# A GFNet filter and MLP on one core: the first layer's result read once from PSUM, and a reordered last step

## The chip, the core and the metric

The kernel runs on one core of one Trainium2 chip. Its engines are TensorE (PE; the weight loads are listed as PEld), VectorE (DVE), ScalarE (ACT), GpSimd (POOL) and the queue engine SyncE (SP), which issues the DMAs. The metric is the device time of one execution in microseconds (us); lower is better.

## The reference

`x` has 2048 rows of 576 numbers in float32. What must be computed is a residual spectral filter, then a residual MLP:

```python
h  = x + irfft2(rfft2(layernorm(x)) * (w_r + 1j * w_i))      # over rows and columns
h2 = h + relu(layernorm(h) @ w1) @ w2                        # w1: 576 x 4608, w2: 4608 x 576
```

## The kernel before

The first part, up to about 270 us, does the Fourier filter as matrix products. The change does not touch it. The second part is the MLP. Its rows are split into `NC` = 4 groups (c) of 512 rows, and its 4608 hidden columns into `NG` = 18 groups (g) of 256. One pair (g, c) is a step; there are 72, in the order of `steps`. Every step adds its part of the second layer to `xs` (tile A in the profile), which holds h and becomes the output.

Full precision is kept by splitting: a number v is written as a high part h (rounded to the matmul type fp32r) and a low part l = v - h, and a product takes three matmuls (h by h, h by l, l by h). The helper `split(h, l, v)` does this with an ACT copy (L151) and a DVE subtraction (L307). `relu_split` (L534) does it straight from PSUM, with the ReLU: an ACT read (L536) and a DVE operation that reads PSUM too (L537).

From step 8 (`WINO`) on, the second layer of a step uses a Strassen-Winograd scheme with seven products instead of eight, of 256 x 128 by 128 x 288 blocks. The hidden block is 256 columns by 512 rows: `p0` and `p1` are its two 128-column halves, after the ReLU, each with 512 rows in two blocks of 256. The left operands are A11 = `p0[:, 0]`, A12 = `p1[:, 0]`, A22 = `p1[:, 1]`, and the sums S1 to S4, which POOL computes from p0 and p1 (L547, L551 to L553). Each left operand is split.

`slot(i)` writes out step i of this kind. TensorE's order is: quarter 0, products A11 and A12, quarter 1, products S2 and S1, quarter 2, products S3 and S4, quarter 3, product A22. A quarter is seven matmuls of the first layer of the *next* step (`mm1`, L148), so that the next step's hidden block is ready when this step ends; after quarters 1 and 3, `hid_a` (L542) reads the finished half from PSUM and starts the sums. A product is six matmuls (`prod`, L562), and after each of them DVE adds the sum so far into one or two blocks of `xs` (`add`, L569).

PSUM holds four tiles `wps`. `wps[0]` takes the products A11, S2, S3 and A22, one summed upon the other, with an add after each; `wps[1]` takes A12, then S1 and S4 upon each other. `wps[2]` and `wps[3]` hold the first layer's halves p0 and p1, one step in the lower and the next in the upper 512 columns. A product that opens or continues a sum in a tile waits for the add that last read this tile.

The kernel's order is written by hand: each engine executes its instructions in the order in which the program lists them, and semaphores join the engines. The second half of `hid_a` stands in quarter 3, thus ahead of the A22 product and its add; in DVE's queue the low part of A12 stands ahead of the A22 add. The last group of hidden columns also stores the output: `store` issues two DMAs on SP for every finished quarter block.

Of the kernel before, what the change touches and what calls it, by code (L numbers as in the profile page):

```python
# [12 lines left out]
AF = mybir.ActivationFunctionType  # L13
ALU = mybir.AluOpType
# [9 lines left out]
CH = 4  # L24
# [103 lines left out]
def kernel(ctx: ExitStack, tc: tile.TileContext, x, w_r, w_i, w1, w2, cc2, c1, fb, ib, c3, out):  # L128
    nc = tc.nc
# [3 lines left out]
    def sb(shape, tag, bufs=1, dt=F32):  # L133
        n[0] += 1
        return pool.tile(shape, dt, tag=tag, name=f"{tag}_{n[0]}", bufs=bufs)

    n = [0]

    def ps():
        n[0] += 1  # L140
        return psum.tile([128, 1024], F32, tag="d", name=f"d_{n[0]}", bufs=4)
# [8 lines left out]
    def act(o, i, **kw):  # L150
        nc.scalar.activation(o, i, AF.Copy, **kw)  # L151

    xs = sb([128, NT, D], "X")
    xv = x[0].rearrange("(h j t) d -> j h t d", j=2, t=NT)
    ov = out[0].rearrange("(h j t) d -> j h t d", j=2, t=NT)
# [149 lines left out]
    def split(h, l, v):  # L305
        act(h, v)
        nc.vector.tensor_sub(l, v, h)  # L307
# [3 lines left out]
    def work(k):  # L311
        for _ in range(k):
            split(*pieces.pop(0))
# [75 lines left out]
    xs = sb([128, NT, D], "A")  # L389
# [70 lines left out]
    def mm1(i, a, part=None):  # L460
        g, c = steps[i]
        w1h, w1l = wts[g, 0]
        if a == 0 and not part:
            pend[i] = None if i >= WINO else ps()
        p = hid_p(i, a) if i >= WINO else pend[i][:, 512 * a:512 * a + 512]
        f = slice(128 * a, 128 * a + 128)
        ops = []
        for kt in range(4):
            ops += [(w1h, kt, kt), (w1h, kt, 5 + kt), (w1l, kt, kt)]
        ops += [(w1h, 4, 4), (w1l, 4, 4)]  # L470
        for n_, (w, kt, xk) in enumerate(ops):
            if part is None or n_ // 7 == part:
                mm(p, w[:, kt, f], xc[c][:, xk, :], n_ == 0, n_ == len(ops) - 1)
        if i >= WINO:
            return
        if a == GF - 1:
            p = pend.pop(i).rearrange("p (a s) -> p a s", a=GF)
            hh, hl = sb([128, GF, 512], "D", 4, F32R), sb([128, GF, 512], "D", 4, F32R)
            nc.scalar.activation(hh, p, AF.Relu)
            nc.vector.scalar_tensor_tensor(hl, p, 0.0, hh, op0=ALU.max, op1=ALU.subtract)  # L480
            hid[i] = (hh, hl)
# [22 lines left out]
    wps, fs = [], {}  # L504
    NAMES = ("B22", "T4", "B11", "B21", "T2", "T1", "T3")

    def wform(n):
        o = 6208 + 576 * NAMES.index(n)
        return tail[0][:, o:o + 288], tail[0][:, o + 288:o + 576]

    def wino_sums(g, *ns):
        v = raw[g][1]
        if 1 in ns:
            T = ebuf([128, 4, 288])
            fs["T1"], fs["T2"], fs["T3"], fs["T4"] = (T[:, i] for i in range(4))
            fs["B11"], fs["B12"], fs["B21"], fs["B22"] = v[:, 0, :288], v[:, 0, 288:], v[:, 1, :288], v[:, 1, 288:]
        for n_ in ns:
            o, a, b = (("T1", "B12", "B11"), ("T2", "B22", "T1"), ("T3", "B22", "B12"), ("T4", "B21", "T2"))[n_ - 1]
            nc.gpsimd.tensor_sub(fs[o], fs[a], fs[b])

    def wino_w(*names):
        for n in names:
            split(*wform(n), fs[n])
# [7 lines left out]
        fs.update(S12f=(D3[:, 0:2], D3[:, 2:4]), S1f=(D3[:, 0], D3[:, 2]), S2f=(D3[:, 1], D3[:, 3]))  # L531
        fs.update(S3f=(tail[0][:, 5696:5952], tail[0][:, 5952:6208]))

    def relu_split(f, p):  # L534
        h, l = f
        nc.scalar.activation(h, p, AF.Relu)  # L536
        nc.vector.scalar_tensor_tensor(l, p, 0.0, h, op0=ALU.max, op1=ALU.subtract)  # L537

    def hid_p(i, k):
        return wps[2 + k][:, 512 * (i % 2):512 * (i % 2) + 512]  # L540

    def hid_a(i, k):  # L542
        p = hid_p(i, k)
        if k == 0:
            relu_split(fs["A11"], p[:, :256])
            nc.scalar.activation(fs["p0"], p.rearrange("p (a n) -> p a n", a=2), AF.Relu)  # L546
            nc.gpsimd.tensor_sub(fs["S3"], fs["p0"][:, 0], fs["p0"][:, 1])  # L547
        else:
            relu_split(fs["A12"], p[:, :256])
            nc.scalar.activation(fs["p1"], p.rearrange("p (a n) -> p a n", a=2), AF.Relu)  # L550
            nc.gpsimd.tensor_add(fs["S1"], fs["p0"][:, 1], fs["p1"][:, 1])  # L551
            nc.gpsimd.tensor_sub(fs["S2"], fs["S1"], fs["p0"][:, 0])  # L552
            nc.gpsimd.tensor_sub(fs["S4"], fs["p1"][:, 0], fs["S2"])  # L553

    def prod(i, a, b, bank, first):
        ah, al = fs[a]
        bh, bl = wform(b)
        P = wps[bank].rearrange("p (a n) -> p a n", a=2)[:, :, :288]
        for tt in range(2):
            q = slice(128 * tt, 128 * tt + 128)  # L560
            for n_, (l, r) in enumerate(((ah, bh), (ah, bl), (al, bh))):
                nc.tensor.matmul(P[:, tt], l[:, q], r, start=first and n_ == 0, stop=n_ == 2, skip_group_check=not first)  # L562

    def add(i, bank, *to):
        c = steps[i][1]
        P = wps[bank].rearrange("p (a n) -> p a n", a=2)[:, :, :288]
        for hs, hd in to:
            xt = xs[:, CH * c + 2 * hs:CH * c + 2 * hs + 2, 288 * hd:288 * hd + 288]
            nc.vector.tensor_add(xt, xt, P)  # L569

    def store(c, hs, hd):
        if steps[-1][0] == NG - 1:
            for j in range(2):
                t, d = CH * c + 2 * hs, slice(288 * hd, 288 * hd + 288)
                nc.sync.dma_start(ov[j, :, t:t + 2, d], xs[64 * j:64 * j + 64, t:t + 2, d])

    def slot(i):
        g, c = steps[i]
        more, last, turn = i + 1 < len(steps), g == NG - 1, c == NC - 1 and g < NG - 1
        new, w1 = c == 0 and g > 2, g < NG - 1 and c in (1, 2)  # L580

        def quarter(k):
            if more:
                mm1(i + 1, k // 2, k % 2)
                if k % 2:
                    hid_a(i + 1, k // 2)

        quarter(0)
        if new:
            wino_w("T3", "B22")  # L590
        if w1:
            work(1)
        prod(i, "A11", "B11", 0, True)
        add(i, 0, (0, 0))
        prod(i, "A12", "B21", 1, True)
        split(*fs["S12f"], fs["S12"])
        add(i, 1, (0, 0))
        if w1:
            wino_sums(g + 1, *((1, 3) if c == 1 else (2, 4)))
        if last:  # L600
            store(c, 0, 0)
        quarter(1)
        prod(i, "S2f", "T2", 0, False)
        add(i, 0, (0, 1))
        split(*fs["S4f"], fs["S4"])
        prod(i, "S1f", "T1", 1, True)
        add(i, 1, (1, 1))
        if turn:
            wino_w("B11", "B21")
        if w1:  # L610
            work(1)
        if new:
            wino_w("T4")
        quarter(2)
        prod(i, "S3f", "T3", 0, False)
        add(i, 0, (1, 1))
        if last:
            store(c, 1, 1)
        if more:
            split(*fs["S3f"], fs["S3"])  # L620
        prod(i, "S4f", "B22", 1, False)
        add(i, 1, (0, 1))
        if turn:
            wino_w("T2", "T1")
        if w1 and c == 1:
            work(1)
        if last:
            store(c, 0, 1)
        quarter(3)
        prod(i, "A22", "T4", 0, False)  # L630
        add(i, 0, (1, 0))
        if more:
            relu_split(fs["A22"], hid_p(i + 1, 1)[:, 256:])
        if last:
            store(c, 1, 0)

    first = [(0, 0), (0, 1), (0, 2), (1, 0), (1, 1), (0, 3), (1, 2), (1, 3)]
    steps = first + [(g, c) for g in range(2, NG) for c in range(NC)]

    gen = None  # L640
    for t in range(NT + 6):
# [15 lines left out]
        if 10 <= t < 22:  # L657
            i, u = divmod(t - 10, 4)
# [15 lines left out]
    for i in range(3, len(steps)):  # L674
        if i + 5 < len(steps) and steps[i + 5] == (steps[i + 5][0], 0):
            load_weights(steps[i + 5][0])
        if i + 3 < len(steps) and steps[i + 3] == (steps[i + 3][0], 0):
            split_weights(steps[i + 3][0], 0)
        if i == WINO - 3:
            wino_sums(2, 1, 2, 3, 4)  # L680
        if i == WINO - 2:
            wino_w("B11", "B21", "T2", "T1", "T3")
        if i == WINO - 1:
            wps += [None, None, ps(), ps()]
            wino_tiles()
        if i == WINO:
            wps[:2] = ps(), ps()
        if i >= WINO:
            slot(i)
            continue  # L690
        for a in range(GF):
            mm1(i + 1, a)
            if i == WINO - 1:
                hid_a(i + 1, a)
        for tt in range(CH):
            mm2(i, tt)
        if i == WINO - 1:
            relu_split(fs["A22"], hid_p(i + 1, 1)[:, 256:])
            split(*fs["S3f"], fs["S3"])
            wino_w("B22", "T4")  # L700

# [21 lines left out]
```

## Time and profile before

| | |
|---|---|
| median of 3 runs | 1055.14 us (1054.94 to 1055.36) |
| profiled execution, its own time | 1053.18 us |
| its span, first to last instruction | 1051.1 us, granted TensorE clock 0.999 |
| TensorE busy | 1033.6 us (98%) |
| DVE busy | 751.3 us (71%) |
| ACT busy | 389.9 us (37%) |
| POOL busy | 325.7 us (31%) |

In the rows of the timeline the columns are: start in us from the span's start, length in us, engine, line, operation, tiles (out <- in), shapes, count, and in brackets the idle time of the engine before the row and what ended it. In the groups of instructions the numbers behind the bar are busy time in us and the mean of one in ns, and behind the next bar the idle time before them. A row of the table of windows has the stretch, its length and the busy time of each engine. PEld rows are the weight loads that go with the matmuls. The tile letters are the program's tags: A is `xs`, d any PSUM tile, D the split left operands, X the split weights and S3's parts, e the float32 tiles p0, p1, S1 to S4 and the raw weights, B and C the first layer's right operand.

### The profile page before, as it was taken

To read this page: it belongs to the slowest core of one execution; us is meant where nothing else is said; L and a number is where in the kernel's file an instruction comes from. 1 tells how busy PE (TensorE), PEld (TensorE's weight loads), DVE (VectorE), ACT (ScalarE), POOL (GpSimd) and SP (SyncE) were. 2 spreads that over 40 slices of the span, in tenths; PEclk is the share of its full clock that TensorE was granted. 3 is DMA by queue.
4 is the path that set the end of the run, shared out by engine and by line. 5 is a ranking of instruction groups with operands and counts; after the bars stand their busy time and mean duration, and the time that the engine had idled before them with its cause. 6 is when DMAs were issued, how large, how long until landed. Compare 5 with 4: busy or idle time off the path is not lost.

```text
span 1051.1 us, 17190 instructions
## 1 busy us (share of the span) xinstructions
PE 1033.6 (98%) x6560; PEld 924.6 (88%) x6560; DVE 751.3 (71%) x1411; ACT 389.9 (37%) x846; POOL 325.7 (31%) x436
## 2 busy tenths in 40 slices
PE   8999999999999999999999999999999999999997
PEld 7878778799999999999999999999999999999996
DVE  7587686544377777778777777778777777777775
ACT  4533243521134333333333333334343333434332
POOL 4300164311132324333333423333333323243321
PEclk9999999999999999999999999999999999999999
DMA  8931700011000110000000011000000001000025
GB/s 241 249 89 49 181 2 26 23 48 49 1 26 23 28 47 23 26 23 26 23 26 23 26 30 42 26 23 26 24 26 23 26 24 46 29 23 2 1 63 118
DMA packets 31073, 48.05 MB, mean 46 GB/s; under 512 B 2960, under 2 KB 22672, under 8 KB 30992
## 3 DMA queue, kind: packets, MB, share of 16 engines
q1 hardware_dynamic: 30992, 46.96, 16.3%
q8 instruction: 52, 0.85, 0.3%
q14 instruction: 29, 0.24, 0.1%
HBM read 42.23 MB, written 4.72 MB: 45 GB/s over the span
## 4 chain that ended last, share of the span: by engine, by line
PE 94%; DVE 2%; DMA 2%; ACT 1%; POOL 0%; issue 0%; SPq 0%; ACTq 0%; DVEq 0%; POOLq 0%
PE d L148 59%; PE d L562 34%; DMA A<-in_A_x_dram 2%; PE d L446 1%; DVE st L208 0%; DVE A L428 0%; ACT e L222 0%; DMA X<-in_A_x_dram 0%; SPq L159 0%; DVE e L307 0%; POOL r L212 0%; DVE e L252 0%; PE d L447 0%; DVE e L253 0%; DVE e L416 0%
## 5 line engine op out<-in xcount | busy, mean ns | idle before, releaser
L569 DVE TENSOR_TENSOR A<-A,d 128x576 f32<-128x576 f32 x448 | 334.5, 747 | 50.5 <-PE d L562 50.2
L562 PE MATMUL d<-X,D 128*128 128x288 f32 x2304 | 346.2, 294 | 1.4 <-DVE A L569 0.9
L562 PEld LDWEIGHTS d<-X,D 128*128 128x128 f32 x2304 | 329.0, 188 | 17.2 <-DVE A L569 1.1
L148 PE MATMUL d<-B,e 128*128 128x512 f32 x952 | 238.3, 391 | 0.4 <-DVE A L428 0.4
L148 PEld LDWEIGHTS d<-B,e 128*128 128x128 f32 x952 | 172.0, 188 | 28.7 <-ACT e L151 0.8
L537 DVE SCALAR_TENSOR_TENSOR D<-d,D 128x256 fp32r<-128x256 f32 x192 | 81.5, 424 | 122.0 <-ACT D L536 122.0
L536 ACT ACTIVATE D<-d 128x256 fp32r<-128x256 f32 x192 | 73.4, 382 | 239.6 <-PE d L148 239.6
L551 POOL TENSOR_TENSOR e<-e 128x256 f32<-128x256 f32 x64 | 47.3, 739 | 355.3 <-ACT e L550 355.3
L148 PE MATMUL d<-C,e 128*128 128x512 f32 x476 | 119.1, 390 | 0.0
L148 PE MATMUL d<-X,e 128*128 128x512 f32 x476 | 118.8, 390 | 0.0
L151 ACT ACTIVATE X<-e 128x288 fp32r<-128x288 f32 (+2 forms) x177 | 70.2, 434 | 105.6 <-PE d L562 105.6
L307 DVE TENSOR_TENSOR D<-e,D 128x512 fp32r<-128x512 f32 (+1 forms) x128 | 92.7, 724 | 19.9 <-ACT D L151 19.9
L547 POOL TENSOR_TENSOR e<-e 128x256 f32<-128x256 f32 x64 | 47.6, 744 | 173.6 <-ACT e L546 173.6
L148 PEld LDWEIGHTS d<-X,e 128*128 128x128 f32 x476 | 85.9, 188 | 13.7
L148 PEld LDWEIGHTS d<-C,e 128*128 128x128 f32 x476 | 85.8, 188 | 13.7
L151 ACT ACTIVATE D<-e 128x512 fp32r<-128x512 f32 (+1 forms) x128 | 66.7, 521 | 75.5 <-POOL e L552 71.9
L307 DVE TENSOR_TENSOR X<-e,X 128x288 fp32r<-128x288 f32 (+2 forms) x177 | 83.1, 492 | 0.9 <-ACT X L151 0.9
L562 PEld LDWEIGHTS d<-X 128*128 128x128 f32 x384 | 58.0, 188 | 5.1
L562 PE MATMUL d<-X 128*128 128x288 f32 x384 | 61.4, 295 | 0.0
L148 PE MATMUL d<-e,D 128*128 128x288 f32 x384 | 53.8, 297 | 0.3 <-DVE D L480 0.3
L148 PEld LDWEIGHTS d<-e,D 128*128 128x128 f32 x384 | 52.2, 188 | 1.4 <-DVE D L480 0.6
L552 POOL TENSOR_TENSOR e<-e,e 128x256 f32<-128x256 f32 x64 | 50.4, 788 | 5.0
(79 smaller groups left out, 986.9 us busy)
## 6 DMA issues: line engine op xcount, KB each, us to landing
e<-in_B_w_dram SPq DMA_DIRECT2D x18, 576.0 KB, 3.8
e<-in_B_w_dram SPq DMA_DIRECT2D x18, 512.0 KB, 3.6
A<-in_A_x_dram SPq DMA_DIRECT2D x16, 288.0 KB, 8.4
out_dram<-A SPq DMA_DIRECT2D x32, 144.0 KB, 2.5
X<-in_A_x_dram SPq DMA_DIRECT2D x12, 288.0 KB, 7.1
e<-in_B_w_dram SPq DMA_DIRECT2D x36, 64.0 KB, 3.4
B<-in_A_w_r_dram SPq DMA_DIRECT2D x15, 144.5 KB, 8.1
B<-in_A_w_i_dram SPq DMA_DIRECT2D x15, 144.5 KB, 7.0
```

What stands on the lines that cost most here:

```text
L148: nc.tensor.matmul(o, l, r, start=start, stop=stop)
L151: nc.scalar.activation(o, i, AF.Copy, **kw)
L307: nc.vector.tensor_sub(l, v, h)
L446: nc.tensor.transpose(pz[:, 128 * b:128 * b + 128], y[:, 128 * b:128 * b + 128], ident)
L536: nc.scalar.activation(h, p, AF.Relu)
L537: nc.vector.scalar_tensor_tensor(l, p, 0.0, h, op0=ALU.max, op1=ALU.subtract)
L547: nc.gpsimd.tensor_sub(fs["S3"], fs["p0"][:, 0], fs["p0"][:, 1])
L551: nc.gpsimd.tensor_add(fs["S1"], fs["p0"][:, 1], fs["p1"][:, 1])
L552: nc.gpsimd.tensor_sub(fs["S2"], fs["S1"], fs["p0"][:, 0])
L562: nc.tensor.matmul(P[:, tt], l[:, q], r, start=first and n_ == 0, stop=n_ == 2, skip_group_check=not first)
L569: nc.vector.tensor_add(xt, xt, P)
```

## The change

Three things change.

1. The first layer's result is read from PSUM once per half. `hid_a` now lets ACT write p0 (or p1), all 512 columns with the ReLU, and A11 and A12 are split from that SBUF tile with `split`; A22 likewise, later in the step. `relu_split` is gone.
2. In the step before the last (`late`), quarter 3 stands directly behind quarter 2, ahead of the S3, S4 and A22 products; the splits of A22 and S3 for the last step stand at its end.
3. In the last step the products that went to `wps[0]` go to `wps[2]` (`X = 2`). Its last add is made in two halves, each with two stores of its own, so four stores of half the size take the place of two.

```diff
-    def relu_split(f, p):
-        h, l = f
-        nc.scalar.activation(h, p, AF.Relu)
-        nc.vector.scalar_tensor_tensor(l, p, 0.0, h, op0=ALU.max, op1=ALU.subtract)
...
         if k == 0:
-            relu_split(fs["A11"], p[:, :256])
             nc.scalar.activation(fs["p0"], p.rearrange("p (a n) -> p a n", a=2), AF.Relu)
+            split(*fs["A11"], fs["p0"][:, 0])
             nc.gpsimd.tensor_sub(fs["S3"], fs["p0"][:, 0], fs["p0"][:, 1])
         else:
-            relu_split(fs["A12"], p[:, :256])
             nc.scalar.activation(fs["p1"], p.rearrange("p (a n) -> p a n", a=2), AF.Relu)
+            split(*fs["A12"], fs["p1"][:, 0])
...
-    def add(i, bank, *to):
+    def add(i, bank, *to, tt=slice(0, 2)):
...
+        late, X = i + 2 == len(steps), 0 if i + 1 < len(steps) else 2
...
-        prod(i, "A11", "B11", 0, True)
-        add(i, 0, (0, 0))
+        prod(i, "A11", "B11", X, True)
+        add(i, X, (0, 0))
...
         quarter(2)
-        prod(i, "S3f", "T3", 0, False)
-        add(i, 0, (1, 1))
+        if late:
+            quarter(3)
+        prod(i, "S3f", "T3", X, False)
+        add(i, X, (1, 1))
         if last:
             store(c, 1, 1)
-        if more:
+        if more and not late:
             split(*fs["S3f"], fs["S3"])
...
-        quarter(3)
-        prod(i, "A22", "T4", 0, False)
-        add(i, 0, (1, 0))
+        if not late:
+            quarter(3)
+        prod(i, "A22", "T4", X, False)
         if more:
-            relu_split(fs["A22"], hid_p(i + 1, 1)[:, 256:])
-        if last:
-            store(c, 1, 0)
+            add(i, X, (1, 0))
+            split(*fs["A22"], fs["p1"][:, 1])
+            if last:
+                store(c, 1, 0)
+            if late:
+                split(*fs["S3f"], fs["S3"])
+        else:
+            for tt in range(2):
+                add(i, X, (1, 0), tt=slice(tt, tt + 1))
+                for j in range(2):
+                    t = CH * c + 2 + tt
+                    nc.sync.dma_start(ov[j, :, t, :288], xs[64 * j:64 * j + 64, t, :288])
```

What this does to the instruction streams is shown at three places. In the names, `D_2581` holds the parts of A11 and A12, `D_2582` those of A22 and S4, `D_2583` those of S1 and S2; `X_1872` holds S3's; `e_2584` is p0 and p1, `e_2585` S1 to S4; `d_2688`, `d_2689`, `d_2579` and `d_2580` are `wps[0]` to `wps[3]`; `A_1268` is `xs`.

ACT at the boundary from slot 69 to slot 70, before and after (the first row is S3's split of slot 69):

```order
L151 ACTIVATE X_1872<-e_2585 128x256
L536 ACTIVATE D_2581<-d_2580 128x256
L550 ACTIVATE e_2584<-d_2580 128x512
L536 ACTIVATE D_2582<-d_2580 128x256
L151 ACTIVATE D_2583<-e_2585 128x512
```
```order
L151 ACTIVATE X_1872<-e_2585 128x256
L544 ACTIVATE e_2584<-d_2580 128x512
L151 ACTIVATE D_2581<-e_2584 128x256
L151 ACTIVATE D_2582<-e_2584 128x256
L151 ACTIVATE D_2583<-e_2585 128x512
```

The long read of p1 now stands ahead of A12's high part, which reads p1 in place of PSUM; A22's high part reads p1 too.

DVE at the same boundary, before and after, from the S4 add of slot 69 to the A11 add of slot 70 and the S1/S2 split behind it:

```order
L569 TENSOR_TENSOR A_1268<-A_1268,d_2689 128x2x288
L537 SCALAR_TENSOR_TENSOR D_2581<-d_2580,D_2581 128x256
L569 TENSOR_TENSOR A_1268<-A_1268,d_2688 128x2x288
L537 SCALAR_TENSOR_TENSOR D_2582<-d_2580,D_2582 128x256
L569 TENSOR_TENSOR A_1268<-A_1268,d_2688 128x2x288
L307 TENSOR_TENSOR D_2583<-e_2585,D_2583 128x512
```
```order
L564 TENSOR_TENSOR A_1268<-A_1268,d_2689 128x2x288
L307 TENSOR_TENSOR D_2581<-e_2584,D_2581 128x256
L564 TENSOR_TENSOR A_1268<-A_1268,d_2688 128x2x288
L307 TENSOR_TENSOR D_2582<-e_2584,D_2582 128x256
L564 TENSOR_TENSOR A_1268<-A_1268,d_2688 128x2x288
L307 TENSOR_TENSOR D_2583<-e_2585,D_2583 128x512
```

The places are the same; the low parts of A12 and A22 are now subtractions with two SBUF inputs.

DVE in the last two steps, before and after, from the S1 add of slot 70 to the S1/S2 split of slot 71:

```order
L569 TENSOR_TENSOR A_1268<-A_1268,d_2689 128x2x288
L569 TENSOR_TENSOR A_1268<-A_1268,d_2688 128x2x288
L307 TENSOR_TENSOR X_1872<-e_2585,X_1872 128x256
L569 TENSOR_TENSOR A_1268<-A_1268,d_2689 128x2x288
L537 SCALAR_TENSOR_TENSOR D_2581<-d_2580,D_2581 128x256
L569 TENSOR_TENSOR A_1268<-A_1268,d_2688 128x2x288
L537 SCALAR_TENSOR_TENSOR D_2582<-d_2580,D_2582 128x256
L569 TENSOR_TENSOR A_1268<-A_1268,d_2688 128x2x288
L307 TENSOR_TENSOR D_2583<-e_2585,D_2583 128x512
```
```order
L564 TENSOR_TENSOR A_1268<-A_1268,d_2689 128x2x288
L307 TENSOR_TENSOR D_2581<-e_2584,D_2581 128x256
L564 TENSOR_TENSOR A_1268<-A_1268,d_2688 128x2x288
L564 TENSOR_TENSOR A_1268<-A_1268,d_2689 128x2x288
L564 TENSOR_TENSOR A_1268<-A_1268,d_2688 128x2x288
L307 TENSOR_TENSOR D_2582<-e_2584,D_2582 128x256
L307 TENSOR_TENSOR X_1872<-e_2585,X_1872 128x256
L564 TENSOR_TENSOR A_1268<-A_1268,d_2579 128x2x288
L307 TENSOR_TENSOR D_2583<-e_2585,D_2583 128x512
```

A12's low part (D_2581) has moved ahead of the S3, S4 and A22 adds of slot 70, and S3's split behind them. TensorE's order changes alike: in slot 70 the seven matmuls of quarter 3 follow quarter 2 directly. At the end of SP's queue the last two stores become four (30 of the old kind, 4 of half the size, where there were 32).

More of the change, by code (lines that the diff above doesn't have):

```diff
@@ L562, in prod @@
                 nc.tensor.matmul(P[:, tt], l[:, q], r, start=first and n_ == 0, stop=n_ == 2, skip_group_check=not first)
-    def add(i, bank, *to):
+    def add(i, bank, *to, tt=slice(0, 2)):
         c = steps[i][1]
-        P = wps[bank].rearrange("p (a n) -> p a n", a=2)[:, :, :288]
+        P = wps[bank].rearrange("p (a n) -> p a n", a=2)[:, tt, :288]
         for hs, hd in to:
-            xt = xs[:, CH * c + 2 * hs:CH * c + 2 * hs + 2, 288 * hd:288 * hd + 288]
+            xt = xs[:, CH * c + 2 * hs:CH * c + 2 * hs + 2, 288 * hd:288 * hd + 288][:, tt]
             nc.vector.tensor_add(xt, xt, P)
@@ L602, in slot @@
         quarter(1)
-        prod(i, "S2f", "T2", 0, False)
-        add(i, 0, (0, 1))
+        prod(i, "S2f", "T2", X, False)
+        add(i, X, (0, 1))
         split(*fs["S4f"], fs["S4"])
@@ L697 @@
         if i == WINO - 1:
-            relu_split(fs["A22"], hid_p(i + 1, 1)[:, 256:])
+            split(*fs["A22"], fs["p1"][:, 1])
             split(*fs["S3f"], fs["S3"])
```

## The prediction

> **What bounds the kernel now.** I read the page's busy shares first (TensorE 98%, in the table above), then busy time by stretch, then the chain that ended last, then one step boundary row by row. Two stretches (four steps from the middle, and the last 13.5 us; after the length come the busy times of TensorE, its weight loads, DVE, ACT and POOL), and two rows of the chain, one step apart:
>
> ```profile
> 347.60:395.30 47.70, 47.70 (x283) 43.29 (x282) 36.13 (x65) 18.25 (x44) 16.24 (x21) 1.00 0.10 27
> 1037.60:1051.10 13.50, 6.99 (x42) 5.82 (x42) 6.80 (x11) 1.54 (x4) 2.20 (x3) 0.94 0.54 128
> ```
> ```profile
> 1013.22 1.60 PE d L148 x7
> 1025.13 1.60 PE d L148 x7
> ```
>
> In the middle TensorE never stops (47.70 of 47.70 us) and a step takes 11.91 us of its work (1025.13 less 1013.22), so nothing saved on ACT, DVE or POOL there can shorten the kernel; a delay that reaches TensorE lengthens it, once per step. In the last stretch TensorE is half idle, and only there can a gain be had. So two questions: does the new first-layer reading keep TensorE fed, and what does the new ending give?
>
> **The boundary between two steps.** The timeline from slot 69 into slot 70, from the end of the fourth quarter on:
>
> ```profile
> 1024.43 0.38 ACT L536 ACTIVATE D<-d 128x256 fp32r<-128x256 f32 x1 [2.09 <-PE d L148]
> 1024.84 1.46 PEld L148 LDWEIGHTS d<-X,e 128*128 128x128 f32 x7
> 1024.85 0.42 DVE L537 SCALAR_TENSOR_TENSOR D<-d,D 128x256 fp32r<-128x256 f32 x1 [1.10 <-ACT D L536]
> 1024.97 1.76 PE L148 MATMUL d<-X,e 128*128 128x512 f32 x7
> 1025.19 0.74 DVE L569 TENSOR_TENSOR A<-A,d 128x576 f32<-128x576 f32 x1
> 1025.31 0.60 ACT L550 ACTIVATE e<-d 128x512 f32<-128x512 f32 x1 [0.49 <-DVE D L537]
> 1025.80 0.38 ACT L536 ACTIVATE D<-d 128x256 fp32r<-128x256 f32 x1
> 1025.99 0.74 POOL L551 TENSOR_TENSOR e<-e 128x256 f32<-128x256 f32 x1 [5.60 <-ACT e L550]
> 1026.21 0.42 DVE L537 SCALAR_TENSOR_TENSOR D<-d,D 128x256 fp32r<-128x256 f32 x1 [0.28 <-ACT D L536]
> 1026.34 1.74 PEld L562 LDWEIGHTS d<-X,D 128*128 128x128 f32 x12
> 1026.57 1.75 PE L562 MATMUL d<-X,D 128*128 128x288 f32 x12
> 1026.80 0.73 POOL L552 TENSOR_TENSOR e<-e,e 128x256 f32<-128x256 f32 x1
> ```
>
> The reader is to see a chain with little room. DVE's add at 1025.19 is the A22 add; it empties bank tile 0, and the first product of the next step (A11, the weight load at 1026.34) opens a new sum in that tile. The add ends at 1025.93: 0.41 us of room. Ahead of this add in DVE's queue stands the low half of A12 (1024.85). After the change it still stands there, but it now waits for a longer chain: ACT reads all 512 columns (p1), ACT copies a half to the high part, and only then DVE subtracts.
>
> **Change 1: one PSUM read, then a split from SBUF.** It removes three short ACT reads and three DVE operations with a PSUM input per step, and adds three ACT copies and three DVE subtractions with both inputs in SBUF. Busy time hardly moves. What moves is when A12's subtraction ends, and there POOL comes in. Groups of DVE and ACT between 300 and 1014 us, then the timeline where S4's subtraction meets a POOL operation:
>
> ```profile
> L307 DVE TENSOR_TENSOR D<-e,D 128x256 fp32r<-128x256 f32 x60 | 46.0, 766 | 18.6 <-ACT D L151 18.6
> ...
> L307 DVE TENSOR_TENSOR X<-e,X 128x256 fp32r<-128x256 f32 x60 | 25.1, 418 | 0.0
> ```
> ```profile
> L151 ACT ACTIVATE D<-e 128x256 fp32r<-128x256 f32 x60 | 24.5, 408 | 0.0
> ```
> ```profile
> 1019.64 0.74 POOL L547 TENSOR_TENSOR e<-e 128x256 f32<-128x256 f32 x1 [3.19 <-ACT e L546]
> 1019.90 0.76 DVE L307 TENSOR_TENSOR D<-e,D 128x256 fp32r<-128x256 f32 x1 [0.31 <-ACT D L151]
> 1020.59 0.74 DVE L569 TENSOR_TENSOR A<-A,d 128x576 f32<-128x576 f32 x1
> ```
>
> The same subtraction takes 418 ns with POOL quiet and 766 ns when it starts inside a POOL subtraction: it ends 0.28 us after POOL does (1020.66 against 1020.38). The operation removed (L537, one input in PSUM) keeps its 0.42 us at 1026.21 although POOL is busy. So the change puts a DVE operation that POOL can hold up in the place of one that it can't.
>
> Worked out for this boundary: p1 can start where A12's read starts now, 1024.43, and takes 0.60: 1025.03. POOL's S1 follows 0.08 later (1025.91 to 1025.99 now): 1025.11 to 1025.85. The ACT copy runs about 1025.09 to 1025.50, so DVE's subtraction arrives inside S1 and ends 0.28 after it: 1026.13, where it ended at 1025.27. The add starts 0.07 before that end (as 1020.59 against 1020.66): 1026.06, and with 0.74 ends 1026.80. TensorE starts 0.06 after such an add, and what a stalled start looks like is in the timeline of the last step:
>
> ```profile
> 1037.10 0.74 DVE L569 TENSOR_TENSOR A<-A,d 128x576 f32<-128x576 f32 x1
> ...
> 1037.90 1.66 PEld L562 LDWEIGHTS d<-X,D 128*128 128x128 f32 x12 [1.09 <-DVE A L569]
> 1037.90 1.89 PE L562 MATMUL d<-X,D 128*128 128x288 f32 x12 [0.85 <-DVE A L569]
> ```
>
> So the weight load goes from 1026.34 to 1026.86, 0.52 late. A stalled start makes up 0.09: from load to the end of twelve matmuls 1.89 us here, 1.98 (1026.34 to 1028.32) in flow. Net 0.43 us. TensorE runs in order and has no slack to take it back. The boundary comes 62 times in this form (slots 8 to 69 of the program; slot 70 is rewritten, 71 is last): 62 x 0.43 = 26.7 us.
>
> Bounds. Below: if POOL did not hold DVE, the subtraction would run 1025.53 to 1025.95, the load 0.34 late, net 0.25: 15.5 us. Above: if DVE had to let S2 pass too (1025.93 to 1026.66), it would end at 1026.94, net 1.24: 77 us. Where two POOL operations follow each other, from DVE's and from POOL's timeline:
>
> ```profile
> 335.58 1.40 DVE L307 TENSOR_TENSOR X<-e,X 128x288 fp32r<-128x288 f32 x2
> ```
> ```profile
> 335.83 0.84 POOL L552 TENSOR_TENSOR e<-e,e 128x256 f32<-128x256 f32 x1
> 336.75 0.84 POOL L553 TENSOR_TENSOR e<-e,e 128x256 f32<-128x256 f32 x1
> ```
>
> DVE ends at 336.98, 0.31 after the first POOL operation, and the second one is stretched to 0.84. DVE slips in between, so I take 26.7. The Trainium skill, page "SBUF — State Buffer", section "Who interferes with whom", says that a DVE instruction with two SBUF inputs contends with a GpSimd instruction that reads SBUF, and that the later one blocks until the first is finished. The trace agrees that it is held up, but taken to the letter the rule would start all 0.42 us at 1025.85, 0.14 later than by the row, which makes an estimate of 62 x 0.14 = 8.7 us more, near 1092; the row decides.
>
> The first half (p0, A11) has the same lengthening. Its ACT read, and the S4 product that it could delay, in the timelines of ACT and TensorE:
>
> ```profile
> 1018.09 0.38 ACT L536 ACTIVATE D<-d 128x256 fp32r<-128x256 f32 x1 [1.80 <-PE d L148]
> ```
> ```profile
> 1021.80 0.95 PE L562 MATMUL d<-X,D 128*128 128x288 f32 x6
> ```
>
> p0 ends 1018.69, S3 on POOL 1018.77 to 1019.51, A11's subtraction 1019.79, the S2 add 1019.72 to 1020.46, S4's subtraction (now clear of POOL) 1020.39 to 1020.81, the S1 add to 1021.47. The S4 product, which needs that add's tile, loads its weights about one matmul (0.95 over six, less the last one's 0.3: 0.13) ahead of 1021.80: 1021.67. Cost zero, with 0.14 us of cover; if the cover is short by 0.1, 6 us more. A22's copy and subtraction lie behind the add and in front of nothing urgent: zero. POOL's S2 and S4 come about 0.9 earlier: zero, since S12's products don't wait in the middle.
>
> **Change 2: the ending.** Rows of the last two steps now: TensorE, DVE, the store queue, and the chain's last row:
>
> ```profile
> 1034.50 1.75 PE L148 MATMUL d<-X,e 128*128 128x512 f32 x7
> 1036.09 0.96 PE L562 MATMUL d<-X,D 128*128 128x288 f32 x6
> ...
> 1040.16 0.54 PE L562 MATMUL d<-X,D 128*128 128x288 f32 x2 [0.36 <-ACT D L151]
> 1040.88 1.73 PE L562 MATMUL d<-X,D 128*128 128x288 f32 x10 [0.19 <-DVE D L307]
> ```
> ```profile
> 1040.14 0.69 DVE L307 TENSOR_TENSOR D<-e,D 128x512 fp32r<-128x512 f32 x1 [0.36 <-ACT D L151]
> ```
> ```profile
> 1045.04 3.30 SPq L575 DMA_DIRECT2D out_dram<-A  x5
> ```
> ```profile
> 1045.52 0.75 DVE A L569
> ```
>
> The waits that it aims at sum to 0.85 + 0.36 + 0.19 = 1.40 us. The fourth quarter moves ahead of two products, about 1.59 us earlier (two products take as long as a quarter, and a quarter is 1036.09 less 1034.50). A12's read would start at 1036.34 now (one step after 1024.43); so p1 starts at about 1034.76, S1 ends 1036.18, A12's subtraction 1036.46. But S3's, S4's and A22's adds now queue behind it: the S3 add ends 1037.13, and the A22 product, which sums into the same tile, loads at 1037.19 where it had run at 1036.09. The A11 product follows without a wait (other tile), near 1038.1, 0.2 later than now. DVE then has the A22 add (1038.29 to 1039.04), two subtractions (0.34 each, as from 1024.85 to 1025.19), the A11 add and only then S12's subtraction, at 1040.32 where it is 1040.14 now. From there the old chain runs on 0.2 late: TensorE's wait has become DVE's queue. Last, the final store is four DMAs in place of two. SP issues its last DMAs back to back (five in 3.30 us, 0.66 each; the last add ends at 1046.27 and two are still to come), so two more cost 1.3 us. Sum +1.5; bounds -1.4 (all three waits gone and the DMAs free) to +2.0.
>
> **Sum.** 26.7 + 1.5 = 28.2 on the profiled span of 1051.1: 1079.3. That execution took 1053.18 in all; the median is 2.0 above it, so 1055.14 + 28.2 = 1083.3 us.
>
> **Rivals.** (a) POOL does not hold DVE: 1055.1 + 15.5 + 1.5 = 1072; against it the 766 ns of all 60. (b) DVE waits for two POOL operations, or a second stall opens at the S4 product: from 1092 to 1133; against it the rows at 335.58 and the 0.14 of cover. (c) Not slower: the A22 add still beats the A11 load. It decides at the end of A12's subtraction: 1026.34 - 0.06 - 0.74 + 0.07 = 1025.61. The ACT read and copy alone end at about 1025.50, so it would need a subtraction of 0.1 us; nothing in the rows is that short. It would leave the ending alone: 1053.7 to 1056.6. (d) The ending does not come out as worked (the earlier quarter is worth nothing, or the two extra stores are hidden): only the boundary term counts, 1081.8, inside the forecast.
>
> **How the numbers follow.** Forecast 0.78 with (d), own range 1078 to 1092; (a) 0.08; (b) 0.06; (c) 0.08, about half of it beyond 0.2% below, since an ending that also packs its products tighter could give over 2.1 us. What differs by less than 0.2% (2.1 us) can't be told from no change here. The range runs from (a) with the ending's better bound to the forecast with the whole 0.14: 1070 to 1092. Faster 0.04, same 0.04, slower 0.92.
>
> **What would show it.** In the profile after: TensorE waiting on DVE's add (now L564) 62 times with some 0.5 us each, a step of 12.34 us instead of 11.91, the 128x256 subtractions into D near 0.75 us where POOL runs, ACT no longer waiting 0.49 on DVE, and the last four stores issued one behind the other, some 0.66 us apart. It is wrong if TensorE is still 100% busy in the middle, or if the waits are near 0.3 or over 1.2 us.

## The result and the profile after

The changed kernel takes 1078.83 us (median of 6 runs, 1077.08 to 1079.08) against 1055.04 for the kernel before (6 runs): a ratio of 1.0222, 95% interval 1.0209 to 1.0235. The profiled execution took 1077.10 us with a span of 1075.3; its span is 24.2 us longer than the one before. Ratios here and below leave out one execution of 5167 us, in which TensorE was several times slower throughout; it is one of ten of the run with the add ahead.

Four steps of the middle and the last 13.5 us in the table of windows, then TensorE's waits between 290 and 1050 us (its weight loads carry them; in the kernel before the same question between 280 and 1030 has no row for TensorE):

```profile
360.00:409.13 49.13, 48.80 (x281) 43.00 (x281) 36.28 (x64) 18.68 (x45) 17.25 (x21) 1.00 0.09 26
1061.82:1075.32 13.50, 6.12 (x38) 4.98 (x37) 6.92 (x13) 0.90 (x3) 0.00 (x0) 0.83 0.61 147
```
```profile
PEld d L557 <- DVE A L564: 22.6, 47, 0.5
PEld d L557 <- ACT X L151: 8.2, 15, 0.5
```

62 waits of half a microsecond, one for each step boundary: 47 put down to DVE's add, and 15, in the slots that also split T3 and B22, to an ACT operation. That operation ended 0.45 us before these 15 loads, though, and they too begin right behind the end of the add (0.12 us, against 0.05 in the other 47), so it is the add that all 62 wait for. The boundary from slot 69 into slot 70, the place that the prediction worked out:

```profile
1047.08 0.60 ACT L544 ACTIVATE e<-d 128x512 f32<-128x512 f32 x1 [2.03 <-PE d L148]
1047.55 1.46 PEld L148 LDWEIGHTS d<-X,e 128*128 128x128 f32 x7
1047.67 1.76 PE L148 MATMUL d<-X,e 128*128 128x512 f32 x7
1047.71 0.72 ACT L151 ACTIVATE D<-e 128x256 fp32r<-128x256 f32 x2
1047.76 0.74 POOL L546 TENSOR_TENSOR e<-e 128x256 f32<-128x256 f32 x1 [5.60 <-ACT e L544]
1048.16 0.62 DVE L307 TENSOR_TENSOR D<-e,D 128x256 fp32r<-128x256 f32 x1 [1.70 <-ACT D L151]
1048.57 0.81 POOL L547 TENSOR_TENSOR e<-e,e 128x256 f32<-128x256 f32 x1
1048.70 0.74 DVE L564 TENSOR_TENSOR A<-A,d 128x576 f32<-128x576 f32 x1
1049.36 0.41 DVE L307 TENSOR_TENSOR D<-e,D 128x256 fp32r<-128x256 f32 x1
1049.41 0.63 ACT L151 ACTIVATE D<-e 128x512 fp32r<-128x512 f32 x1 [0.98 <-POOL e L547]
1049.46 0.92 POOL L548 TENSOR_TENSOR e<-e,e 128x256 f32<-128x256 f32 x1
1049.49 1.65 PEld L557 LDWEIGHTS d<-X,D 128*128 128x128 f32 x12 [0.48 <-DVE A L564]
1049.49 1.88 PE L557 MATMUL d<-X,D 128*128 128x288 f32 x12
```

Read from the top: the long read of p1 ends at 1047.68, POOL's S1 runs from 1047.76 to 1048.50, DVE's subtraction for A12 comes in at 1048.16 and takes 0.62 where 0.42 is its length alone. It ends at 1048.78, 0.28 after S1. The A22 add stands behind it and ends at 1049.44; the next product's weights load at 1049.49. In the kernel before they loaded 1.37 us after quarter 0's first matmul (1024.97 to 1026.34); here that would have been 1049.04.

The ending: the third quarter of slot 70 in the kernel before, then rows of the timeline after from this quarter on:

```profile
1031.32 1.75 PE L148 MATMUL d<-X,e 128*128 128x512 f32 x7
```
```profile
1054.40 3.34 PE L148 MATMUL d<-X,e 128*128 128x512 f32 x14
...
1058.86 0.62 DVE L307 TENSOR_TENSOR D<-e,D 128x256 fp32r<-128x256 f32 x1 [2.48 <-ACT D L151]
...
1060.19 2.46 PEld L557 LDWEIGHTS d<-X,D 128*128 128x128 f32 x18 [1.10 <-DVE A L564]
1060.19 2.69 PE L557 MATMUL d<-X,D 128*128 128x288 f32 x18 [0.87 <-DVE A L564]
...
1063.31 0.68 DVE L307 TENSOR_TENSOR D<-e,D 128x512 fp32r<-128x512 f32 x1
```
```profile
1060.17 9.98 SPq L570 DMA_DIRECT2D out_dram<-A  x12
1070.25 2.47 SPq L642 DMA_DIRECT2D out_dram<-A  x4
```

This quarter began at 1031.32 before, so up to here the loss is 23.1 us. 0.2 of it is there before the first of the 62 boundaries (the matmuls of quarter 1 of slot 8 begin at 289.70 against 289.52); 22.9 / 62 = 0.37 us for each boundary. From here to the end the kernel needs 20.9 us where it needed 19.7: another 1.2. TensorE's wait of 0.87 is still there; it has moved one product ahead, to the A22 product at 1060.19, and the four half stores are issued last, one behind the other.

### The profile page after: what moved, and what is told of

Read it like the earlier page. It is cut to its first block, busy times and chain, and to the rows that moved or that the text cites. A ratio compares the mean times of both kernels' runs of the same rounds, so it can differ in the third digit from the quotient of the medians.

```text
span 1075.3 us, 17194 instructions
## 1 busy us (share of the span) xinstructions
PE 1051.8 (98%) x6560; PEld 921.1 (86%) x6560; DVE 754.1 (70%) x1412; ACT 396.6 (37%) x846; POOL 341.4 (32%) x436
## 4 chain that ended last, share of the span: by engine, by line
PE 79%; DVE 9%; ACT 7%; DMA 2%; issue 1%; POOL 0%; SPq 0%; DVEq 0%; ACTq 0%; POOLq 0%
PE d L148 49%; PE d L557 30%; DVE A L564 4%; ACT e L544 4%; DVE D L307 3%; ACT D L151 2%; DMA A<-in_A_x_dram 2%; PE d L446 1%; DVE st L208 0%; DVE A L428 0%; ACT e L222 0%; DMA X<-in_A_x_dram 0%; SPq L159 0%; DVE e L307 0%; POOL r L212 0%
## 5 line engine op out<-in xcount | busy, mean ns | idle before, releaser
L557 PEld LDWEIGHTS d<-X,D 128*128 128x128 f32 x2304 | 324.9, 188 | 43.2 <-DVE A L564 23.7
L557 PE MATMUL d<-X,D 128*128 128x288 f32 x2304 | 353.1, 298 | 6.6 <-DVE A L564 3.8
L564 DVE TENSOR_TENSOR A<-A,d 128x576 f32<-128x576 f32 (+1 forms) x449 | 334.1, 745 | 28.4 <-PE d L557 28.2
L307 DVE TENSOR_TENSOR D<-e,D 128x256 fp32r<-128x256 f32 (+1 forms) x320 | 175.4, 548 | 185.1 <-ACT D L151 185.1
L151 ACT ACTIVATE D<-e 128x256 fp32r<-128x256 f32 (+1 forms) x320 | 133.3, 454 | 51.6 <-POOL e L547 41.3
L540 ACT ACTIVATE e<-d 128x512 f32<-128x512 f32 x64 | 38.3, 599 | 197.1 <-PE d L148 197.1
L544 ACT ACTIVATE e<-d 128x512 f32<-128x512 f32 x64 | 38.3, 599 | 116.6 <-PE d L148 116.6
L548 POOL TENSOR_TENSOR e<-e,e 128x256 f32<-128x256 f32 x64 | 58.3, 911 | 5.0
L307 DVE TENSOR_TENSOR e<-e,e 128x256 fp32r<-128x256 f32 (+2 forms) x83 | 53.3, 647 | 0.6 <-issue 0.6
```

## The experiments

Theory A is the prediction's: A12's low half is late (longer ACT chain, and POOL holding DVE), the A22 add waits behind it in DVE's queue, and the A11 product waits for the add. The rivals are named in the expectations. Ratios are against runs of the kernel before on the same chip.

**The single read alone.** The kernel before, with only `hid_a` and the A22 split changed:

```diff
-            relu_split(fs["A12"], p[:, :256])
             nc.scalar.activation(fs["p1"], p.rearrange("p (a n) -> p a n", a=2), AF.Relu)
+            split(*fs["A12"], fs["p1"][:, 0])
```

> The kernel before with the single PSUM read and the splits from SBUF alone; the order of the last step, its PSUM tile and its stores stay as before. Theory A (the low half of A12 ends late and holds up the A22 add, and that holds up the next step's first product): the 62 boundaries cost 0.37 us each as in the changed kernel, 23.1 us, and the boundary into the last step, which already waited 0.85 us, waits some 0.8 longer, of which about 0.4 stays: about 1078.5 us. Theory B (much of the loss comes from the new ending): clearly less than 1077 us.

Measured: 1078.24 us, ratio 1.0222 (1.0207 to 1.0238), the same as the whole change. TensorE's waits between 290 and 1050 us:

```profile
PEld d L562 <- DVE A L569: 22.1, 46, 0.5
PEld d L562 <- ACT X L151: 8.1, 15, 0.5
```

The last of the 62 boundaries lies behind this window. From the first p1 read to the last one it takes 779.2 us against 756.2: 23.0, or 0.37 for each of 62 boundaries. The loss lies in this part; theory B falls.

**The ending alone.** The changed kernel with `relu_split` put back at all three places:

```diff
+            relu_split(fs["A12"], p[:, :256])
             nc.scalar.activation(fs["p1"], p.rearrange("p (a n) -> p a n", a=2), AF.Relu)
-            split(*fs["A12"], fs["p1"][:, 0])
...
-            split(*fs["A22"], fs["p1"][:, 1])
+            relu_split(fs["A22"], hid_p(i + 1, 1)[:, 256:])
```

> The changed kernel with the PSUM reads of before (ACT and DVE both read PSUM) and only the new ending: earlier fourth quarter in the step before the last, other PSUM tile, four half stores. Theory A: no stall in the middle (TensorE idle there under 0.1 us a step); the ending gains some 0.5 us on DVE's chain, since A12's low half comes 0.9 us sooner than in the changed kernel, and loses 1.3 us to two more stores: about 1055.7 us, not to be told from before. Theory B: some 10 us or more above before.

Measured: 1055.34 us, ratio 1.0007 (0.9998 to 1.0017). TensorE waits nowhere in the middle, steps take 11.91 us. The ending in the timeline (the third quarter of slot 70 begins at 1031.43, 0.11 later than before):

```profile
1035.29 0.42 DVE L537 SCALAR_TENSOR_TENSOR D<-d,D 128x256 fp32r<-128x256 f32 x1 [1.94 <-ACT D L536]
...
1036.43 2.41 PEld L562 LDWEIGHTS d<-X,D 128*128 128x128 f32 x18 [0.30 <-DVE A L569]
...
1039.67 0.68 DVE L307 TENSOR_TENSOR D<-e,D 128x512 fp32r<-128x512 f32 x1
```

With A12's low half at 1035.29 the weights of the A22 product wait 0.30 instead of 1.10 (at 1060.19 in the changed kernel), and S12's subtraction comes at 1039.67 where it was 1040.14 before. The reordered step is worth about 0.6 us by itself; the kernel still ends 20.2 us after the third quarter against 19.7, since the stores cost more than that.

**A12 alone from PSUM.** The changed kernel, with `relu_split` for A12 only, ahead of the read of p1:

```diff
-            nc.scalar.activation(fs["p1"], p.rearrange("p (a n) -> p a n", a=2), AF.Relu)
-            split(*fs["A12"], fs["p1"][:, 0])
+            relu_split(fs["A12"], p[:, :256])
+            nc.scalar.activation(fs["p1"], p.rearrange("p (a n) -> p a n", a=2), AF.Relu)
```

> The changed kernel, but A12 alone is split straight from PSUM again, ahead of the read of p1; A11 and A22 come from SBUF. Theory A: A12 is the only one that costs, A11 and A22 are free: no stall at the boundary, about 1055.7 us. Rival C (any of the three splits from SBUF costs its share, for instance A11 through the S4 product): a step stays 0.1 us or more over 11.91, 1062 us or more.

Measured: 1060.54 us, ratio 1.0054 (1.0039 to 1.0069). The stall at the A11 product is gone, as theory A has it, but the middle still loses 6.4 us where nothing was expected. 5.1 of them lie in the 15 slots that split T3 and B22, which take 12.24 to 12.30 us; the others take 11.91 to 11.98. DVE and POOL in one such slot:

```profile
336.02 0.62 DVE L307 TENSOR_TENSOR D<-e,D 128x256 fp32r<-128x256 f32 x1 [0.41 <-ACT D L151]
336.56 1.91 DVE L307 TENSOR_TENSOR X<-e,X 128x288 fp32r<-128x288 f32 x2
338.39 0.74 DVE L569 TENSOR_TENSOR A<-A,d 128x576 f32<-128x576 f32 x1
339.05 0.68 DVE L307 TENSOR_TENSOR D<-e,D 128x512 fp32r<-128x512 f32 x1
```
```profile
335.62 0.74 POOL L551 TENSOR_TENSOR e<-e 128x256 f32<-128x256 f32 x1 [6.48 <-ACT e L550]
336.44 0.80 POOL L552 TENSOR_TENSOR e<-e,e 128x256 f32<-128x256 f32 x1
337.31 0.84 POOL L553 TENSOR_TENSOR e<-e,e 128x256 f32<-128x256 f32 x1
```
```profile
339.79 1.35 PEld L562 LDWEIGHTS d<-X,D 128*128 128x128 f32 x9 [0.17 <-DVE D L307]
```

A22's subtraction (0.62 for 0.42) and the two of T3 and B22 (1.91; in the run with the ending alone the same two take 1.40) each meet one of POOL's three sums. S12's subtraction ends at 339.73, and the S2 product waits for it. Rival C is right in part: splits from SBUF other than A12's can cost too, though by this queue and not through the S4 product.

**The low half from PSUM, the high half from SBUF.** One operand of the changed kernel, A12's low half:

```diff
-            split(*fs["A12"], fs["p1"][:, 0])
+            act(fs["A12"][0], fs["p1"][:, 0])
+            nc.vector.scalar_tensor_tensor(fs["A12"][1], p[:, :256], 0.0, fs["A12"][0], op0=ALU.max, op1=ALU.subtract)
```

> The changed kernel with one operand exchanged: A12's high half is still copied from p1 in SBUF, behind the long ACT read, but its low half is taken by DVE from PSUM (one SBUF input instead of two). The length of ACT's chain is the same; only POOL can no longer hold the subtraction up. Theory A with POOL's part: the subtraction ends about 0.18 us sooner, the step takes 12.10 us instead of 12.28, total about 1067.5 us. Rival D (only the longer ACT chain counts, POOL does not matter): no change, 1078.8 us.

Measured: 1066.14 us, ratio 1.0108 (1.0093 to 1.0123); steps of 12.05 to 12.16 us. The boundary into slot 70 in the timeline:

```profile
1038.34 0.74 POOL L547 TENSOR_TENSOR e<-e 128x256 f32<-128x256 f32 x1 [5.60 <-ACT e L544]
1038.75 0.42 DVE L546 SCALAR_TENSOR_TENSOR D<-d,D 128x256 fp32r<-128x256 f32 x1 [1.70 <-ACT D L151]
1039.09 0.75 DVE L565 TENSOR_TENSOR A<-A,d 128x576 f32<-128x576 f32 x1
...
1039.89 0.69 PEld L558 LDWEIGHTS d<-X,D 128*128 128x128 f32 x5 [0.29 <-DVE A L565]
```

The operation starts at the same place in the chain, inside POOL's S1, and now takes 0.42 instead of 0.62. From the first p1 read to the last, with the 1.6 us added by which the last one comes earlier in both, the changed kernel loses 22.8 us to the kernel before and this one 11.3. So of the 0.37 us at a boundary half is POOL holding DVE (11.5 us in all, 0.18 each) and half the longer ACT chain. Rival D falls.

**The add ahead.** The changed kernel, with the second half's reading and splits moved behind the A22 add, except in slot 70:

```diff
-                if k % 2:
+                if k % 2 and (k == 1 or late):
                     hid_a(i + 1, k // 2)
...
             add(i, X, (1, 0))
+            if not late:
+                hid_a(i + 1, 1)
             split(*fs["A22"], fs["p1"][:, 1])
```

> The changed kernel with one thing moved: in every slot but the one before the last, the A22 add stands ahead of the second half's ACT read and splits in the program, so that DVE's queue no longer has A12's low half in front of the add. All operations stay. Theory A (the add waits behind A12's low half, nothing else): the stall at the A11 product is gone in all 62 boundaries. What the run with A12 from PSUM showed comes in: in the 15 slots that also split T3 and B22, the SBUF subtractions queue up against POOL and the S2 product waits some 0.2 to 0.35 us. So a step takes 11.92 us and those 15 up to 12.25: 1 to 5 us over the run with the ending alone, about 1058 us. Rival (the single read costs by its length wherever the add stands): 1070 us or more.

Measured: 1054.61 us, ratio 1.0004 (0.9995 to 1.0013). Since its profile shows nothing of the steps, it was run again:

> The kernel with the A22 add ahead, once more, since its first profile fell into an execution in which TensorE ran several times slower throughout and shows nothing of the steps. Theory A: no wait of TensorE for an add at the 62 boundaries; steps of 11.91 us, in the 15 slots with the T3 and B22 splits at most 0.3 more; the ending as in the changed kernel, 20.9 us from the third quarter of slot 70.

Measured: 1055.84 us, ratio 1.0013 (1.0003 to 1.0023). TensorE has no wait between 290 and 1036 us, every step takes 11.91 us, and the ending is 20.9 us long. One boundary of it, with the T3 and B22 splits:

```profile
336.37 0.75 DVE L564 TENSOR_TENSOR A<-A,d 128x576 f32<-128x576 f32 x1 [0.64 <-PE d L557]
336.84 0.76 ACT L151 ACTIVATE X<-e 128x288 fp32r<-128x288 f32 x2
337.04 1.29 DVE L307 TENSOR_TENSOR D<-e,D 128x256 fp32r<-128x256 f32 x2
337.07 0.99 POOL L547 TENSOR_TENSOR e<-e,e 128x256 f32<-128x256 f32 x1
337.55 1.73 PEld L557 LDWEIGHTS d<-X,D 128*128 128x128 f32 x12
```

All operations of the change are there, the subtractions still meet POOL (1.29 for two, and POOL's S2 stretched to 0.99), and it costs nothing, since the add at 336.37 no longer stands behind them. The remark that the 15 slots would lose up to 0.3 was wrong here: POOL's S1 starts 0.08 us after quarter 0's first matmul and not 0.96 after it, as in the run with A12 from PSUM (335.62 against 334.66 there), and S12's subtraction is in time. With every operation of the change kept, the whole loss of the middle goes away with the place of one add in a queue.

**Whole stores.** The run with the ending alone, without the last add's halves:

```diff
-            for tt in range(2):
-                add(i, X, (1, 0), tt=slice(tt, tt + 1))
-                for j in range(2):
-                    t = CH * c + 2 + tt
-                    nc.sync.dma_start(ov[j, :, t, :288], xs[64 * j:64 * j + 64, t, :288])
+            add(i, X, (1, 0))
+            store(c, 1, 0)
```

> The run with the ending alone, its last add made whole again and followed by two stores of full size instead of four of half. By the prediction's store term (0.66 us for each DMA that SP issues behind the last add) the last issue ends some 1.3 us sooner and the span is 1.2 us shorter than with the four: about 1054.1 us. Rival (the halves overlap with the add and cost nothing): the span stays or grows.

Measured: 1054.33 us, ratio 0.9996 (0.9987 to 1.0005). The spans differ in their first part (the third quarter of slot 70 begins 1.5 us later here than in the run with the ending alone), so the ending is compared from that quarter on: 19.2 us against 20.2 with the halves, 1.1 sooner; the last issue ends 16.4 us after it instead of 17.7. The store term holds.

**Two queues.** Every second store of the last three blocks issued by ACT:

```diff
-                nc.sync.dma_start(ov[j, :, t:t + 2, d], xs[64 * j:64 * j + 64, t:t + 2, d])
+                (nc.scalar if two and j else nc.sync).dma_start(ov[j, :, t:t + 2, d], xs[64 * j:64 * j + 64, t:t + 2, d])
```

> As the run with whole stores, and the last step's last three blocks are stored by two queues: one of the two DMAs of each block from SP, the other from ACT, which has nothing left to do there. SP's backlog should be gone: the last issue ends 0.6 us after the last add instead of about 2. Span some 1.3 us shorter than with whole stores on SP, about 1052.5 us, some 0.2% under before. Rival (issue was not what set the end, the landing of the last DMA does): no shorter than with whole stores.

Measured: 1053.67 us, ratio 0.9992 (0.9983 to 1.0001). Stores at the end, of the run with whole stores and of this one:

```profile
1045.44 3.94 SPq L575 DMA_DIRECT2D out_dram<-A  x6
```
```profile
1045.57 2.58 ACTq L575 DMA_DIRECT2D out_dram<-A  x3
```

The last issue ends 1.35 us sooner, as expected, but the kernel only 0.7 (18.5 us after the third quarter): from the last issue to the end it takes 3.4 us instead of 2.7. The rival was half right. The longer wait lies in the DMAs: from issue to landing the last six take 2.5 us (median) on one queue, and 2.8 on SP and 3.2 on ACT with two. Why they take longer was not tried.

**The ending packed.** With two queues, and S3's split of the last step behind that of S1 and S2:

```diff
-            if late:
-                split(*fs["S3f"], fs["S3"])
...
         add(i, 1, (0, 0))
+        if not more:
+            split(*fs["S3f"], fs["S3"])
```

> The run with two store queues, and in the last step the split of S3 stands behind that of S1 and S2 (it is needed two products later). DVE's queue reaches the A11 add and the S1/S2 split some 0.4 us sooner, so the last add ends about 14.0 us after the third quarter of slot 70 begins instead of 14.37 and the kernel ends at about 18.1 instead of 18.47. Against before, which ends at 19.74: 1.6 us, 0.15%, at the edge of what the timing can tell. Rival (TensorE or the products' order sets the ending by then): the last add stays at 14.4.

Measured: 1053.17 us, ratio 0.9985 (0.9976 to 0.9994): the one version whose interval lies below 1, by 0.15%, which is less than the 0.2% that the prediction held to be distinguishable. The last add ends 13.96 us after the third quarter begins (14.37 before this edit), the kernel 18.2 after it against 19.7 in the kernel before.

## Why the prediction was right

The forecast was 1083 us in a range of 1070 to 1092; 1078.83 was measured. On two rows rests what is said of its second step below, the first matmuls of the fourth quarter of slot 69, before and after:

```profile
1022.58 1.75 PE L148 MATMUL d<-C,e 128*128 128x512 f32 x7
```
```profile
1045.29 1.75 PE L148 MATMUL d<-C,e 128*128 128x512 f32 x7
```

Its steps:

- *TensorE waits for the add 62 times, about 0.5 us each.* Shown: 62 waits, 30.8 us together, 0.5 each. The chain is the one worked out: p1, S1, subtraction 0.28 after S1, add, weight load.
- *0.43 us net for a boundary, 26.7 in all.* Mis-sized: 0.37 and 22.9. The term that failed is "p1 can start where A12's read starts now". Before, A12's ACT read began 1.85 us after its quarter's first matmul (1022.58 to 1024.43); p1 begins 1.79 after it (1045.29 to 1047.08). That is 0.06 us, 3.7 us over 62 boundaries, against a difference of 3.8. Why the read starts sooner stays open; its length is not the reason, since in the run with A12 from PSUM A12's short read, too, begins 1.79 us after its quarter. From 1047.08 on the sum of the terms holds to 0.02 us (2.41 us to the weight load, 2.43 worked out).
- *POOL holds the subtraction up until 0.28 after its own end.* Shown by the rows after, and by the exchange of one operand, which gave 0.18 of 0.37 back, as expected. The Trainium skill, page "SBUF — State Buffer", section "Who interferes with whom", says that a DVE instruction with at most one SBUF input, outside the two-port performance modes, does not contend with GpSimd; the 0.42 us at 1038.75 agrees. The letter of its rule for two inputs, a wait for the end of the POOL instruction, would have given 0.42 after S1 instead of 0.28; the row decided rightly. The sign "near 0.75 us where POOL runs" did not come true: A12's subtraction took 0.62, and the working itself has 0.60 (1025.53 to 1026.13); 0.76 was the length of one that met POOL earlier in POOL's operation.
- *DVE slips in between two POOL operations.* Shown: S2 follows S1 at 1048.57 and the subtraction ends at 1048.78; S2 is stretched to 0.81.
- *A11's longer chain costs nothing at the S4 product.* Shown: TensorE has no wait there in the changed kernel. *A22 is free* held in the changed kernel and in the one with the add ahead, but not where POOL's sums come late: in the kernel with A12 from PSUM the 15 slots with the T3 and B22 splits lose 0.34 us each.
- *The ending costs 1.5.* It costs 1.2. DVE's S12 subtraction comes 8.91 us after the third quarter begins (1054.40 to 1063.31); forecast 9.00, before 8.82. The four stores end their issue 1.3 us later than two did. Not counted was that with half-size DMAs last the kernel ends 0.1 us sooner after its last issue (2.59 us against 2.73).
- The rivals: POOL not holding DVE (1072), two POOL operations ahead (from 1092) and no loss (1054 to 1057) are all excluded by the rows at 1047 to 1049. The fourth, an ending that counts for nothing (1081.8), falls with the 1.2 us measured there.

## What to carry to other kernels

Reading a PSUM tile once and splitting from SBUF saves no time on an engine that does not bound, and it makes the first operand later by a whole read. When an operation is made later or held up by another engine, look at what stands behind it in its own queue: here an add that frees the accumulator of the bounding engine, and moving that add one place ahead took back 23 us with no operation changed. Before cutting a last store into pieces, look whether its queue still has issues waiting; each piece adds one (0.6 us each here).

## What was not expected of the hardware

Taking half of the last stores to a second queue ended the issues 1.35 us sooner and the kernel only 0.7, since each then took longer to land. POOL is stretched as well when it meets DVE: S2 takes 0.73 us alone, 0.81 behind one subtraction and 0.99 behind two.
